# Small transform units made inside the matmul stretch of a last-stage chunk, in mid-step

## The chip, the cores and the metric

The kernel runs on one core of a Trainium2 chip. The metric is the device time of one execution in microseconds (us); a kernel's number is the median of its runs. A profile is one more execution, recorded instruction by instruction. TensorE (PE) multiplies matrices, VectorE (DVE) and ScalarE (ACT) do elementwise work and read the accumulators (PSUM), GpSimd (POOL) does elementwise work on the on-chip memory (SBUF) and issues DMAs, SyncE (SP) issues DMAs.

## The reference

The input is `x` of shape (8, 3008, 256). Along the sequence axis it is convolved with a filter given in the frequency domain, and the result goes through a two-layer network with a hard-swish:

```python
X = np.fft.rfft(x, axis=1)
y = np.fft.irfft(X * (filt_r + 1j * filt_i)[None], n=3008, axis=1)   # (8, 3008, 256)
h = y.reshape(8 * 3008, 256) @ w_in                                  # 256 -> 2048
out = (h * np.clip(h + 3, 0, 6) / 6) @ w_out                         # 2048 -> 256
```

All of it is float32.

## The kernel before

**The main loop.** The 24064 tokens are cut into 47 blocks of 512, and the 2048 hidden columns into 8 slices. A *step* is one (block, slice) pair; step i is slice i mod 8 of block i // 8, so there are 376. From block 1 on a step is an up projection (`up_1` to `up_5`, seven products of 128x128 by 256 columns, line L764), the activation (`relu` on ScalarE, L809; `hswish` on VectorE, L814), sums of activations (`g_sums` and `g_last`, L821, L822 and L827 on VectorE), and the down projection of the step before (`down`, L843). The products run with fewer multiplications by sums of operands; `t_sums` (L760) makes those sums of a block's tokens with seven GpSimd instructions. Around a block's end the accumulators `po` are combined: `out_1` (ScalarE), `out_2` (L909) and `out_3` (L914) in the step whose number is a multiple of 8, `out_4` (L918, L919 and one GpSimd sum) and `out_5` (L923) in the step after it. `out_3` waits for the last product of its step.

**The order within a step** is written out by hand. After `up_1` comes place 0 of the plan, then `hswish` of the second half of the step before, `g_sums`, `down(1)`, `up_2`, `down(2, 4)`, `up_3`, `down(5, 6)`, `up_4`, then place 1, `hswish` of the first half, `up_5` (with the second `relu`), `bi3_copies`, `down(7, 3)` and place 2. Each engine runs its instructions in the order in which they are written, so what stands earlier in this list also runs earlier on its engine.

**The transforms** of batches 1 to 7 are made beside the main loop, by units that a table `plan` hangs on steps and places:

- First stage: `a6_unit` (L480, place 1) turns six columns c at a time, in three *rounds* of four products; `a6_sums` (L495 to L498, VectorE, place 2) forms sums and differences, and `z6_store` (L505) writes them from GpSimd's queue. A batch has 32 columns: five sixes and a rest of two (`SIX`, `A_AT`). The rest has a single round and its own small tile.
- Second stage: `b_unit` (L539, place 0), `f_unit` (filter, VectorE, place 2), `y_unit` (L571, L572, VectorE with both operands in SBUF, place 2).
- Inverse: `bi3_unit` (place 1) takes three `y` tiles in three rounds (L599); its copies are on ScalarE (L602, L609) and VectorE (L601, L610), and `g3_store` writes from GpSimd's queue.
- Last stage: `n_five` (L704, place 0) makes a *chunk* of five columns with 40 small products, `ring` (L686, ScalarE) copies it into the ring `xn` of tokens, and `ready` calls `t_sums` when a block of tokens is full. `n_unit` makes smaller chunks.

**Quarters.** The products of these units use 64 rows by 64 columns of the array. Four of them, one on each quarter of the array, make a round. [...]In units of three rounds a third tile shares the bank `be`: one row half writes its part in the first round, the other in the third, and a tiny VectorE copy of two elements (L483, L601) stands between them, because the other half's product waits for it. Each float32 product shows as two records in the profile.

`psF` has two banks (the units' `psf` and the chunks' `psn`), `be` and `al` one each; `be` is also used by every step's up projection. `t3p` has one buffer (the three-tile result of `a6_unit` and `bi3_unit`), `t1p` two, `yp` three.

Of the kernel before, what the change touches and what calls it, by code (L numbers as in the profile page):

```python
# [10 lines left out]
FP32 = mybir.dt.float32  # L11
I32 = mybir.dt.int32
AXT = mybir.ActivationFunctionType
ALU = mybir.AluOpType
# [23 lines left out]
HC = NC // 2  # L38
XC = 4
NB = HC // XC  # L40
SIX = tuple(range(0, HC, 6))
TC = 4
NT = KH // TC
TB = 3
# [138 lines left out]
def kernel(  # L183
# [198 lines left out]
    def x_at(b, c):  # L382
        if b == 1:
            return xs[:, (b * NB + c) % 3, :, :], c * XC, XC
        t = xs.rearrange("p i j d -> p (i j) d")
        return t[:, ds((b * len(SIX) + c) % 2 * 6, 6), :], SIX[c], min(6, HC - SIX[c])

    def x_load(b, c):
        t, c0, n_ = x_at(b, c)
# [70 lines left out]
    def a_sums(b, c):  # L460
# [5 lines left out]
        nc.vector.tensor_tensor(out=t[:, :, 1, :], in0=t[:, :, 0, :], in1=ps, op=ALU.subtract)  # L466
        nc.vector.tensor_tensor(out=t[:, :, 0, :], in0=t[:, :, 0, :], in1=ps, op=ALU.add)

    def a6_unit(b, c):
        xc, c0, n = x_at(b, c)  # L470
        n //= 2
        t = t3p.tile([P, 3, 2, D], FP32, name="t3") if n == 3 else t1p.tile([P, 2, 2, D], FP32, name="t1")
        banks = [psF.tile([P, 512], FP32, name="psf", tag="f") for h in range(2)]
        be = psU.tile([P, 512], FP32, name="be") if n == 3 else None
        for r in range(n):
            for g in range(2):
                for h in range(2):
                    j, ps, o = (2, be, h) if r == 2 - 2 * h and n == 3 else (r - h if n == 3 else 0,) + (banks[h], r - h if n == 3 else 0)
                    q = g * n + j
                    nc.tensor.matmul(ps[ts(g, 64), ts(o, D)], wa[ds(h * 64, NA), ds((c0 + q) * 2 * KH, 64)],  # L480
                                     xc[ds(h * 64, NA), q, :], start=True, stop=True)
            if n == 3 and r == 0:
                nc.vector.tensor_copy(out=t[:, 2, 1, 0:2], in_=be[:, D:D + 2])  # L483
        m = min(n, 2)
        two = [ps[:, 0:m * D].rearrange("p (j d) -> p j d", d=D) for ps in banks]
        nc.scalar.activation(out=t[:, 0:m, 0, :], in_=two[0], func=AXT.Copy)
        if n == 3:
                nc.scalar.activation(out=t[:, 2, 1, 2:D], in_=be[:, D + 2:], func=AXT.Copy)
        st["t1", b, c] = t, be, two[1], n

    def a6_sums(b, c):
        t, be, ps, n = st["t1", b, c]
        v, m = nc.vector, min(n, 2)
        if n == 3:
            v.tensor_tensor(out=t[:, 2, 0, :], in0=be[:, 0:D], in1=t[:, 2, 1, :], op=ALU.add)  # L495
            v.tensor_tensor(out=t[:, 2, 1, :], in0=be[:, 0:D], in1=t[:, 2, 1, :], op=ALU.subtract)
        v.tensor_tensor(out=t[:, 0:m, 1, :], in0=t[:, 0:m, 0, :], in1=ps, op=ALU.subtract)
        v.tensor_tensor(out=t[:, 0:m, 0, :], in0=t[:, 0:m, 0, :], in1=ps, op=ALU.add)  # L498

    def z6_store(b, c):  # L500
        t, _, _, n = st.pop(("t1", b, c))
        for g in range(2):
            for ri in range(2):
                p0 = g * 64 + ri * KH
                nc.gpsimd.dma_start(z_d[b, :, ri, ds(SIX[c] + n * g, n), :, :].rearrange("k j s d -> k (j s d)"),  # L505
                                    t[p0:p0 + KH, 0:n, :, :].rearrange("p j s d -> p (j s d)"))

    def z_store(b, c, q=nc.gpsimd):
# [80 lines left out]
    def bi3_unit(b, i):  # L589
        ys = [st.pop(("y", b, i + v)) for v in range(3)]  # L590
        c = psU.tile([P, 512], FP32, name="be")
        banks = [psF.tile([P, 512], FP32, name="psf", tag="f") for ri in range(2)]
        t = t3p.tile([P, 3, 2, D], FP32, name="t3")
        to = [t[:, q, :, :].rearrange("p u d -> p (u d)") for q in range(3)]
        for r in range(3):
            for v in range(2):
                for ri in range(2):
                    x, u, ps, o = (2, v, c, ri) if r == 2 * ri else (v, r - 1 + ri, banks[ri], r - 1 + ri)
                    nc.tensor.matmul(ps[ts(v, 64), ts(o, D)], wi[ts(ri, 64), 0, :], ys[x][ts(ri, 64), u, :], start=True, stop=True)  # L599
            if r == 0:  # L600
                nc.vector.tensor_copy(out=to[2][:, 0:2], in_=c[:, 0:2])  # L601
        nc.scalar.activation(out=to[1], in_=banks[1], func=AXT.Copy)  # L602
        st["t3", b, i] = t
        st["bi3"] = to[0], banks[0], to[2], c

    def bi3_copies():
        if "bi3" in st:
            to, ps, third, c = st.pop("bi3")
            nc.scalar.activation(out=to, in_=ps, func=AXT.Copy)  # L609
            nc.vector.tensor_copy(out=third[:, 2:512], in_=c[:, 2:512])  # L610
# [81 lines left out]
            t_sums(t // PAIRS)  # L692


    def n_five(i):
        b, js, o, n = chunks[i]
        s0 = i % 2 * NJ
        ps = [psF.tile([P, 512], FP32, name="psn", tag="f")[:, 0:2 * n].rearrange("p (e n) -> p e n", e=2) for c in range(2)]
        for q, j in enumerate(js):
            for dh in range(2):  # L700
                for g in range(2):
                    for c in range(2):
                        r = ds(c * HALF, ATOM)
                        nc.tensor.matmul(ps[c][ts(g, HALF), dh, ts(q, NA)], t4[r, s0 + q, ds(dh * P + g * HALF, HALF)],  # L704
                                         groups[r, j, :], start=True, stop=True)
        for c in range(2):
            ring(i, 0, n, o, lambda at_: xn[:, :, c, at_], ps[c])
        ready(i)

    def n_unit(i, dh):  # L710
        ps = psF.tile([P, 512], FP32, name="psn", tag="f")
# [261 lines left out]
    EARLY = (a_unit, b_unit, bi_unit, n_unit, n_five)  # L973

    def at(step, fn, *a):
        plan.setdefault((step, 0 if fn in EARLY else 1 if fn in (w_scale, bi3_unit, a6_unit) else 2), []).append((fn, a))

    with tc.manual_schedule():

# [131 lines left out]
        in_block = {}  # L1111
        for i in range(2, len(chunks)):
            in_block.setdefault(pair(i)[0] // PAIRS, []).append(i)
        stored = 0
        for i in range(2, len(chunks)):
            k = pair(i)[0] // PAIRS
            head = chunks[i][2] == 0
            same = in_block[k]
            at_, kind = same.index(i) + 1 if len(same) > 1 else 0, kinds.get(k - 1, "a")
            steps = N_FIRST[k - 1][at_] if k - 1 in N_FIRST else (FIVE_AT[kind][at_],) * 2 if len(chunks[i][1]) == NJ else N_AT[kind][at_]  # L1120
            if head and len(same) == 1:
                steps = (6, 6)
            s0, s1 = ((k - 1) * NP + s for s in steps)
            five = len(chunks[i][1]) == NJ
            n_at[i] = s1
            if head:
                stored = s0 - 3 + (k == first[1])
            at(max(stored, n_at[i - 2] + 1), t4_load, i)
            if five:
                at(s1, n_five, i)  # L1130
                continue
            at(s0, n_unit, i, 0)
            at(s1, n_unit, i, 1)
# [1 line left out]

        A_AT = (4, 6, 10, 12, 14, 15)

        def places(n):  # L1140
            if n == 1:
                return (list(range(2, NB + 2)), [12, 13, 14, 18, 19, 20, 22, 23, 26, 27, 29, 31],
                        [13, 15, 16, 19, 21, 22, 24, 25, 28, 30, 30, 32], [17, 24, 30, 34])
            k = first[n] * NP
            a_at = [k - 7 * NP + i for i in A_AT]
            f_at, y_at, bi_at = ([k - (5 - 2 * r) * NP + i for r in range(2) for i in p]
                                 for p in ((2, 3, 6, 7, 12, 13), (4, 5, 10, 11, 14, 15), (11, 16)))
            return a_at, f_at, y_at, bi_at

        at(n_at[TAIL - 2] + 1, lambda: nc.sync.dma_start(edge, wai_d[:, ds(NW + ND, ND)]))  # L1150
# [2 lines left out]
        for n in range(1, B):  # L1153
            a_at, f_at, y_at, bi_at = places(n)
            for c, s in enumerate(a_at):
                at(s, a_unit if n == 1 else a6_unit, n, c)
                at(s, a_sums if n == 1 else a6_sums, n, c)
                at(s, *((z_store, n, c, nc.sync) if n == 1 else (z6_store, n, c)))
                if c >= (3 if n == 1 else 2):
                    at(max(a_at[c - 3 + (n > 1)], s - 6), x_load, n, c)  # L1160
                elif n > 1:
                    at(max(prev[-1 if n == 2 else c - 2], s - 6), x_load, n, c)
# [5 lines left out]
            for i in range(NU):  # L1168
                if i % 2 == 0 or n == 1:
                    at(f_at[i], b_unit, n, i)  # L1170
                if i % 3 == 0:
                    at(bi_at[i // 3], bi3_unit, n, i)
                    at(bi_at[i // 3], g3_store, n, i)
                at(y_at[i], y_unit, n, i)
            for i in range(NU):
                at(f_at[i], f_unit, n, i)
            prev = a_at

        HEAVY = (f_unit, y_unit, a_sums, n_five, a6_sums, bi3_unit)

        def late(i):
            return i % NP in (1, 2) or any(fn in HEAVY for place in range(3) for fn, a in plan.get((i - 1, place), ()))
# [103 lines left out]
```

## Time and profile before

| | |
|---|---|
| median of 3 runs | 2643.08 us (2642.48 to 2643.17) |
| the profiled execution | 2642.37 us, of which the span from first to last instruction is 2640.5 us |
| granted TensorE clock | 1.000 |
| busy: PE, DVE, ACT, POOL | 2626.3, 2046.7, 1296.5, 485.5 us |

From the trace's timeline of TensorE one reads the length of each step, from the start of its first up product to that of the next step's. From step 36 on (the steady part):

| what hangs on the step | steps | length, us |
|---|---|---|
| nothing | 207 | 6.148 to 6.149 |
| `b_unit` | 36 | 7.365 |
| `a6_unit`, a six | 18 | 7.879 to 7.883 |
| `a6_unit`, the rest of two | 6 | 6.936 to 6.937 |
| `bi3_unit` | 15 | 7.855 to 7.858 |
| `n_five` | 22 | 7.656 to 7.753 |
| `n_five` and a six | 12 | 9.387 to 9.390 |
| `n_five` and `bi3_unit` | 7 | 9.363 to 9.366 |

Numbers within a step are given as +x us from its start. How a line of the profile reads: line of the kernel, engine, operation, output<-inputs, shape, and count; then busy time and the mean of one, or, in a timeline, start and duration first and in brackets the engine's idle time before it with what ended it.

### The profile page before, as it was taken

What the parts mean: (1) busy time and instruction counts of PE and PEld (TensorE: products, weight loads), DVE (VectorE), ACT (ScalarE), POOL (GpSimd) and SP (SyncE); (2) the same over time, 40 slices, a digit from 0 to 9 for tenths busy, and PEclk for the clock granted to TensorE, in tenths of its full rate; (3) what the DMA queues carried; (4) which work ended last, traced back from release to release, by engine and by line L of the source; (5) the groups of instructions that cost most, each with busy time, mean ns of one, the idle gap of its engine ahead of it and who ended that gap; (6) DMA issues with size and microseconds to landing.
All of it is one profiled execution on the core that took longest, in us unless ns stands there. A gap on an engine that the chain in (4) does not pass through costs nothing.

```text
span 2640.5 us, 54927 instructions
## 1 busy us (share of the span) xinstructions
PE 2626.3 (99%) x21920; PEld 2338.3 (89%) x21920; DVE 2046.7 (78%) x3611; ACT 1296.5 (49%) x2677; POOL 485.5 (18%) x711
## 2 busy tenths in 40 slices
PE   9999999999999999999999999999999999999999
PEld 6698988989889998889988898888988889999998
DVE  7978867887678876788778887788877878766666
ACT  4554454444544445444454544545445454455554
POOL 2242021110211102121021210211112120111110
PEclk9999999999999999999999999999999999999999
DMA  9733234113341123411233112331223321110000
GB/s 247 222 85 83 55 103 112 53 32 85 81 113 53 36 81 85 109 53 36 81 89 105 53 37 80 89 104 53 58 61 88 104 56 48 48 43 23 19 21 25
DMA packets 130710, 198.29 MB, mean 75 GB/s; under 512 B 21602, under 2 KB 97472, under 8 KB 130262
## 3 DMA queue, kind: packets, MB, share of 16 engines
q1 hardware_dynamic: 115165, 150.12, 20.7%
q0 software_dynamic: 14720, 44.16, 6.1%
q8 instruction: 173, 2.83, 0.5%
q14 instruction: 83, 0.68, 0.1%
q10 hardware_dynamic: 569, 0.50, 0.1%
HBM read 122.43 MB, written 83.98 MB: 78 GB/s over the span
## 4 chain that ended last, share of the span: by engine, by line
PE 97%; DMA 1%; DVE 1%; issue 0%; ACT 0%; SPq 0%; POOL 0%; POOLq 0%; DVEq 0%; ACTq 0%
PE po L843 43%; PE al L764 24%; PE be L764 18%; PE psn L704 2%; PE psf L539 1%; PE psf L480 1%; PE po L886 1%; PE psf L599 1%; PE be L599 1%; PE be L480 1%; PE al L875 0%; PE be L875 0%; DMA ft<-in_filt_i_dram 0%; PE psf L453 0%; PE psn L715 0%; DMA wa<-wb_t 0%
## 5 line engine op out<-in xcount | busy, mean ns | idle before, releaser
L843 PEld LDWEIGHTS po<-w_all,g 128*128 128x128 f32 x10276 | 1370.3, 191 | 106.9 <-issue 10.4
L843 PE MATMUL po<-w_all,g 128*128 128x128 f32 x10276 | 1393.9, 276 | 1.0 <-DVE g L814 0.6
L809 ACT ACTIVATE r<-h,half_c 128x512 f32<-128x512 f32 x736 | 531.0, 721 | 334.3 <-DVE h L790 322.3
L764 PE MATMUL al<-xt,w_all 128*128 128x256 f32 x2208 | 659.6, 381 | 0.1
L814 DVE SCALAR_TENSOR_TENSOR g<-r,h 128x512 f32<-128x512 f32 x736 | 533.9, 727 | 147.6 <-ACT r L809 132.4
L764 PE MATMUL be<-xt,w_all 128*128 128x256 f32 x1472 | 437.8, 379 | 0.0
L790 DVE TENSOR_TENSOR h<-be,s 128x512 f32<-128x512 f32 x368 | 253.6, 689 | 144.8 <-PE be L764 136.2
L764 PEld LDWEIGHTS al<-xt,w_all 128*128 128x128 f32 x2208 | 335.4, 192 | 1.0 <-issue 0.5
L760 POOL TENSOR_TENSOR xt<-xn 128x256 f32<-128x256 f32 x184 | 149.7, 833 | 905.8 <-ACT xn L686 905.8
L764 PEld LDWEIGHTS be<-xt,w_all 128*128 128x128 f32 x1472 | 279.7, 190 | 37.9
L804 ACT ACTIVATE h<-al 128x256 f32<-128x256 f32 x368 | 141.4, 384 | 297.3 <-PE al L764 297.3
L795 DVE TENSOR_TENSOR h<-al,s 128x256 f32<-128x256 f32 x368 | 156.0, 424 | 156.2 <-PE al L764 154.3
L822 DVE TENSOR_TENSOR g<-g 128x512 f32<-128x512 f32 x367 | 261.4, 712 | 12.6
L785 ACT ACTIVATE s<-al 128x256 f32<-128x256 f32 x368 | 141.4, 384 | 214.4 <-PE al L764 212.9
L764 PE MATMUL al<-xn,w_all 128*128 128x256 f32 x736 | 226.4, 389 | 0.0
L776 ACT ACTIVATE s<-be 128x256 f32<-128x256 f32 x368 | 141.4, 384 | 171.0 <-PE be L764 171.0
L764 PE MATMUL be<-xn,w_all 128*128 128x256 f32 x736 | 218.9, 379 | 0.0
L821 DVE TENSOR_TENSOR g<-g 128x256 f32<-128x256 f32 x367 | 165.0, 450 | 12.6
L775 ACT ACTIVATE s<-al 128x256 f32<-128x256 f32 x368 | 141.1, 383 | 64.8 <-PE al L764 64.8
L827 DVE TENSOR_TENSOR g<-g 128x256 f32<-128x256 f32 x367 | 160.1, 436 | 2.4
L764 PEld LDWEIGHTS be<-xn,w_all 128*128 128x128 f32 x736 | 139.8, 190 | 18.9
L764 PEld LDWEIGHTS al<-xn,w_all 128*128 128x128 f32 x736 | 111.4, 191 | 24.7 <-issue 22.3
(170 smaller groups left out, 1850.0 us busy)
## 6 DMA issues: line engine op xcount, KB each, us to landing
t<-g_tmp SPq DMA_DIRECT2D x184, 120.0 KB
t<-z_tmp SPq DMA_DIRECT2D x42, 512.0 KB
g_tmp<-t POOLq DMA_DIRECT2D x68, 256.0 KB, 4.3
z_tmp<-t POOLq DMA_DIRECT2D x120, 144.0 KB, 3.5
o_tmp<-o SPq DMA_DIRECT2D x46, 256.0 KB
xs<-in_x_dram SPq DMA_DIRECT2D x60, 192.0 KB
ft<-in_filt_r_dram SPq DMA_DIRECT2D x168, 64.0 KB
ft<-in_filt_i_dram SPq DMA_DIRECT2D x168, 64.0 KB
```

The costliest lines, as they stand in the source:

```text
L760: nc.gpsimd.tensor_tensor(out=o, in0=x0, in1=x1, op=op_)
L764: nc.tensor.matmul(ps, w_in[p][:, w, :], x, start=start, stop=stop, skip_group_check=True)
L776: nc.scalar.activation(out=s5, in_=be[:, 1, :], func=AXT.Copy)
L785: nc.scalar.activation(out=s[:, 1, :], in_=al, func=AXT.Copy)
L790: nc.vector.tensor_tensor(out=st["h"][0].rearrange("p (a n) -> p a n", a=2), in0=be, in1=s, op=ALU.add)
L795: nc.vector.tensor_tensor(out=st["h"][1][:, 256:512], in0=al, in1=s5, op=ALU.add)
L809: nc.scalar.activation(out=r, in_=st["h"][i], func=AXT.Relu, bias=half_c, scale=1.0 / 6.0)
L814: nc.vector.scalar_tensor_tensor(out=st["g", k, p][:, o:o + 2, :].rearrange("p a n -> p (a n)"), in0=st["r", i], scalar=1.0, in1=st["h"][i ...
L821: v.tensor_tensor(out=g[:, G1, :], in0=g[:, G3, :], in1=g[:, G22, :], op=ALU.add)
L822: v.tensor_tensor(out=g[:, G3:G2 + 1:2, :], in0=g[:, G3:G1 + 1, :], in1=g[:, G11:G11 + 1, :].broadcast_to([P, 2, 256]), op=ALU.subtract)
L827: nc.vector.tensor_tensor(out=g[:, G4, :], in0=g[:, G12, :], in1=g[:, G2, :], op=ALU.subtract)
L843: nc.tensor.matmul(st["po", k][bank][:, part, u, :], g[:, a, ts(u, P)], w_out[p][:, w, :], start=(p == 0 and n in OPENS and u == 0), stop= ...
```

## The change

- `SIX` becomes 6, 6, 6, 6, 2, 6. The unit of two columns and, per batch of 2 to 7, three inverse units of a single `y` tile no longer have a stretch of their own: `five_and` makes each of them within the products of a chunk of five. In such a chunk one row half first makes two 256-column products of the small unit while the other row half makes eight products of the chunk; then both halves make twelve; then the roles are exchanged. Both halves of the small unit share the bank `be`, with the tiny VectorE copy (`order`) between.
- `five_and` stands at place 1 (before `up_5`), where the chunk alone stands at place 0. The ring copies, `ready` (and so `t_sums`) and the big VectorE copy of the inverse unit move to `bi3_copies`, behind `up_5`.
- Per batch of 2 to 7, four `bi3_unit` become three, and three single units are new (`BI_AT`). `A_AT` puts the first-stage units on offsets 4, 6, 8, 10, 12, 14 (before: 4, 6, 10, 12, 14, 15) from a step that is a multiple of 8. In the last batch one `y_unit` goes one step later.
- In `a6_unit` and `bi3_unit` the two products of one row half now follow each other within a round, and the half that writes `be` comes first in the first round and last in the third.

```diff
-SIX = tuple(range(0, HC, 6))
+SIX = (0, 6), (6, 6), (12, 6), (18, 6), (24, 2), (26, 6)
...
+    def a_product(ps, g, o, xc, c0, q, h):
+        nc.tensor.matmul(ps[ts(g, 64), ts(o, D)], wa[ds(h * 64, NA), ds((c0 + q) * 2 * KH, 64)],
+                         xc[ds(h * 64, NA), q, :], start=True, stop=True)
+
     def a6_unit(b, c):
...
         for r in range(n):
+            for h in (1, 0):
+                for g in range(2):
+                    j, ps, o = (2, be, h) if r == 2 - 2 * h else (r - h, banks[h], r - h)
+                    a_product(ps, g, o, xc, c0, g * n + j, h)
+            if r == 0:
+                nc.vector.tensor_copy(out=t[:, 2, 1, 0:2], in_=be[:, D:D + 2])
...
+    def a2_parts(b, c):
+        xc, c0, n = x_at(b, c)
+        t = t1p.tile([P, 2, 2, D], FP32, name="t1")
+        be = psU.tile([P, 512], FP32, name="be")
+        st["t1", b, c] = t, be, None, 1
+
+        def part(h):
             for g in range(2):
...
+                a_product(be, g, h, xc, c0, g, h)
+
+        def order():
+            nc.vector.tensor_copy(out=t[:, 0, 1, 0:2], in_=be[:, D:D + 2])
+
+        def copies():
+            nc.scalar.activation(out=t[:, 0, 1, 2:D], in_=be[:, D + 2:], func=AXT.Copy)
+        return 1, part, order, copies, lambda: None
...
         for r in range(3):
-            for v in range(2):
-                for ri in range(2):
+            for ri in range(2):
+                for v in range(2):
...
+    def bi1_parts(b, i):
+        y = st.pop(("y", b, i))
+        t = st["t3", b, i] = t1p.tile([P, 2, 2, D], FP32, name="t1")
+        be = psU.tile([P, 512], FP32, name="be")
...
+        def part(ri):
+            for v in range(2):
+                nc.tensor.matmul(be[ts(v, 64), ts(ri, D)], wi[ts(ri, 64), 0, :], y[ts(ri, 64), v, :], start=True, stop=True)
+
+        def order():
+            nc.vector.tensor_copy(out=to[:, 0:2], in_=be[:, 0:2])
+
+        def copies():
+            nc.vector.tensor_copy(out=to[:, 2:512], in_=be[:, 2:512])
+        return 0, part, order, lambda: None, copies
...
     def bi3_copies():
+        if "five" in st:
+            for f in st.pop("five"):
+                f()
...
-    def n_five(i):
+    def n_five(i, parts=None, b_=0, x=0):
...
+        order = [(q, dh, g) for q in range(NJ) for dh in range(2) for g in range(2)]
...
+        def both(a, b, n):
+            for i in range(n):
+                for c, o in ((0, a), (1, b)):
+                    product_(c, *order[o + i])
+
+        def rings():
+            for c in range(2):
+                ring(i, 0, n, o, lambda at_: xn[:, :, c, at_], ps[c])
+            ready(i)
+
+        if parts is None:
+            both(0, 0, len(order))
+            rings()
+            return
+        r, part, sync, copies, last = parts(b_, x)
+        part(r)
+        for m in range(8):
+            product_(1 - r, *order[m])
+        sync()
+        both(8 * r, 8 - 8 * r, 12)
+        part(1 - r)
+        for m in range(12, 20):
+            product_(r, *order[m])
+        copies()
+        st["five"] = last, rings
+
+    def five_and(*a):
+        n_five(*a)
...
-        A_AT = (4, 6, 10, 12, 14, 15)
+        BI_AT = {2: ((9, 0, 1), (14, 1, 3), (16, 4, 1), (25, 5, 1), (27, 6, 3), (32, 9, 3)),
+                 6: ((9, 0, 1), (14, 1, 3), (16, 4, 1), (17, 5, 1), (27, 6, 3), (32, 9, 3)),
+                 7: ((9, 0, 1), (11, 1, 1), (16, 2, 1), (17, 3, 3), (27, 6, 3), (32, 9, 3))}
+        A_AT = (4, 6, 8, 10, 12, 14)
...
+            bi_at = [(k - 5 * NP + s, i, m) for s, i, m in BI_AT.get(n, BI_AT[2])]
+            y_at[5] += n == B - 1
...
+        for s, i in five_at.items():
+            at(s, *((five_and, i) + with_five[s] if s in with_five else (n_five, i)))
...
-        HEAVY = (f_unit, y_unit, a_sums, n_five, a6_sums, bi3_unit)
+        HEAVY = (f_unit, y_unit, a_sums, n_five, five_and, a6_sums, bi3_unit)
```

## The prediction

> **What bounds the kernel now.** I read the engines' shares first, then the chain of waits, then the costliest groups.
>
> ```profile
> PE 2626.3 (99%) x21920; PEld 2338.3 (89%) x21920; DVE 2046.7 (78%) x3611; ACT 1296.5 (49%) x2677; POOL 485.5 (18%) x711
> PE 97%; DMA 1%; DVE 1%; issue 0%; ACT 0%; SPq 0%; POOL 0%; POOLq 0%; DVEq 0%; ACTq 0%
> L843 PE MATMUL po<-w_all,g 128*128 128x128 f32 x10276 | 1393.9, 276 | 1.0 <-DVE g L814 0.6
> ```
>
> TensorE is busy all the time and makes 97% of the chain. So a change pays by what it takes out of TensorE's row of products, and it costs where a product has to wait. VectorE is at 78%: in a step with added work it can become late. The timeline of TensorE gives a price for each unit; here the step with the unit of two columns:
>
> ```profile
> 736.74 0.60 PE L764 MATMUL al<-xt,w_all 128*128 128x256 f32 x2
> ...
> 741.65 0.66 PE L480 MATMUL psf<-xs,wa 47*64 47x256 f32 x8
> 742.25 0.70 PE L764 MATMUL al<-xn,w_all 128*128 128x256 f32 x2
> ...
> 743.67 0.60 PE L764 MATMUL al<-xt,w_all 128*128 128x256 f32 x2
> ```
>
> The step lasts 6.936 us, a bare one 6.148: the unit costs 0.788. Record by record, a 256-column record occupies its quarter for 0.216, so the round's own work is 0.432; the rest, 0.356, is going into quarters and out again. In the same way a chunk costs 7.656 - 6.148 = 1.508: twenty rounds of records at 0.0583 are 1.166, the rest is 0.342. A chunk and a six in one step cost 3.241 = 1.508 + 1.733: two stretches, paid twice.
>
> **Gains.** (1) Removed per batch of 2 to 7: the unit of two (0.788) and one `bi3_unit` (7.857 - 6.148 = 1.709). Over six batches: 14.98 us.
>
> (2) Added: 24 small units inside chunks. In the first part one half makes two 256-column products (0.432 per quarter) beside eight chunk products, four per quarter, 4 x 2 x 0.0583 = 0.467. Then twelve each, 0.700, then 0.467 again: 1.634 in place of 1.166, so 0.467 more. The lower end is the products' own 0.432. For the upper end there is a rule against the change. The Trainium skill ("TensorE: Matmul & The Clock Gate", The mechanism, in Part 3) says that products start and end strictly in the order of issue. Then the eight products behind two long ones could not start before the second long record, and each part would take 0.22 to 0.27 longer: some 0.95 per unit, 11.6 us more in all. The trace speaks otherwise: in a six's first round the second record of the first quarter starts 0.267 after its first, but the other three quarters start 0.007 to 0.020 after it. A quarter runs behind its own records alone. I take 0.467: 24 x 0.467 = 11.21 us.
>
> (3) Third rounds. In a `bi3_unit` the last rounds' records in `be` start 1.398 after the last full product, their neighbour at 1.335; in a six 1.417 and 1.335. So the wait for the tiny VectorE copy costs 0.063 and 0.082 a unit (lower end of the gain: nothing; upper: all of it). In the new order `be` is first in round one and last in round three, which is two places of 0.0067 for the inverse and four for the six; the weights, not loaded ahead behind a wait (0.051), stay exposed. I take 0.020 and 0.026: 22 x 0.020 + 30 x 0.026 = 1.2 us.
>
> (4) Chunks alone in a step last up to 7.753 because `t_sums` slows the `g_last` in the same step. The converted ones lose this excess over 7.656: 0.4 us.
>
> Gains: 14.98 - 11.21 + 1.2 + 0.4 = 5.4 us.
>
> **Losses.** All come from VectorE and ScalarE getting work later, and each is a wait of TensorE. The price of a wait: with `g_last` ended at +7.104 in step 121, the product due at +7.208 ran 0.051 late, so a product runs 0.155 after its operand. These are the VectorE instructions around a block's end (steps 80 and 81, which starts at 638.09):
>
> ```profile
> 637.40 0.68 DVE L909 TENSOR_TENSOR o<-po,p 128x512 f32<-128x512 f32 x1
> 638.29 0.42 DVE L914 TENSOR_TENSOR o<-po,o 128x256 f32<-128x256 f32 x1 [0.21 <-PE po L843]
> 638.63 0.68 DVE L814 SCALAR_TENSOR_TENSOR g<-r,h 128x512 f32<-128x512 f32 x1
> ...
> 640.42 0.42 DVE L918 TENSOR_TENSOR o<-po,o 128x256 f32<-128x256 f32 x1
> 640.75 0.41 DVE L919 TENSOR_TENSOR o<-po,o 128x256 f32<-128x256 f32 x1
> ```
>
> and these a six's sums, in steps 84 and 85 (from 665.31):
>
> ```profile
> 664.42 0.42 DVE L495 TENSOR_TENSOR t<-be,t 128x256 f32<-128x256 f32 x1 [0.58 <-ACT t L488]
> 664.88 0.42 DVE L496 TENSOR_TENSOR t<-be,t 128x256 f32<-128x256 f32 x1
> 665.22 0.68 DVE L497 TENSOR_TENSOR t<-t,psf 128x512 f32<-128x512 f32 x1
> 665.93 0.69 DVE L498 TENSOR_TENSOR t<-t,psf 128x512 f32<-128x512 f32 x1
> 666.53 0.68 DVE L814 SCALAR_TENSOR_TENSOR g<-r,h 128x512 f32<-128x512 f32 x1
> ```
>
> (5) The new offset 8 in `A_AT` puts a six on a step that is a multiple of 8, where `out_2` and `out_3` stand; none stood there. `out_3` waits for the step's last product and ends at +0.62 of the next step. The sums are queued behind it: 2.12 us from first to last start and the next, so `hswish` starts at +2.66 in place of +0.54 and ends at +3.34. `down(2)`, due at +2.61, runs at 3.50: 0.89 late. `g_sums` ends at 4.5, `out_4` at 5.2, and `down(5)` must not overwrite the `po` that `out_4` reads: it runs at 5.36, due at 3.93 + 0.89 = 4.82, so 0.54 more. The sum for the other half of h comes behind it and holds `up_5` by some 0.05. Together 1.48 per batch: 8.9 us. Cover that remains: none, since the next step has `out_4` and `out_5` of its own.
>
> (6) Ring copies behind the second `relu`. In step 112 that `relu` starts 0.27 before the next step. Ring copies start 0.62 and 1.08 after it, each holding ScalarE 0.46, so the copy of `al` starts at +1.26 (normally +0.63) and ends at +1.64. `up_2` overwrites `al` at +1.74 and needs it ended at 1.59: 0.06 late. It's the same in 22 steps (two have a `b_unit` between); in five the chunk wraps round the ring, with twice the copies and 0.08 more. 1.6 us.
>
> (7) `t_sums` starts behind the ring copies, at +1.4 of the next step instead of +3.9 of the chunk's own. What it does to VectorE, in steps 121 and 122:
>
> ```profile
> 917.55 1.60 POOL L760 TENSOR_TENSOR xt<-xt 128x256 f32<-128x256 f32 x2
> ...
> 917.77 0.79 DVE L827 TENSOR_TENSOR g<-g 128x256 f32<-128x256 f32 x1
> 918.49 2.35 DVE L814 SCALAR_TENSOR_TENSOR g<-r,h 128x512 f32<-128x512 f32 x2
> 920.87 0.83 DVE L821 TENSOR_TENSOR g<-g 128x256 f32<-128x256 f32 x1
> ```
>
> Two SBUF operands cost 0.79 instead of 0.42, and 1.19 instead of 0.69; operands from PSUM aren't slowed. The seven sums last 5.8 to 6.05. Before, step 122 bore this without a wait (6.148 long). Now they end at +7.3, so `g_last` and `hswish` of the step behind the chunk are slowed (`hswish` ends near +6.6), and a `y_unit` at its end too: two instructions of 0.69 become 1.1 each, and the next `hswish` ends at +2.9 of the step after. `down(2)` runs at 3.04, due at 2.61: 0.43. This meets offset 10 in five batches and 26 in four: 9 x 0.43 = 3.9 us. The Trainium skill ("SBUF — State Buffer", SBUF: two separate sides) calls the shared port an exclusive lock, the loser blocked for a whole instruction. A slowed VectorE instruction would then lose up to the 0.73 of a GpSimd sum, not the row's 0.38 to 0.50: four such in a row make 1 us more per place, 9 in all. I take the row. Without a `y_unit` the slowed work has room (`hswish` due by +2.45).
>
> (8) In the last batch `y_unit` 5 moves to step 304, behind `out_2` and `out_3` and into the `t_sums` of a chunk; as in (5), with 1.7 us of `y` ahead of a slowed `hswish`: 2.1 us, once.
>
> Losses: 8.9 + 1.6 + 3.9 + 2.1 = 16.5 us. DMAs: each six still has four steps (over 25 us) between its load and its use, and stores wait some 4 us to land; GpSimd's queue issues two more stores per batch, behind `t_sums`. I put these at nothing.
>
> **Sum.** 16.5 - 5.4 = +11.1 us. On the profiled execution: 2642.37 + 11.1 = 2653.5 (span 2651.6). The median of the runs stands 0.71 above that execution, so 2643.08 + 11.1 = 2654.2. A difference under 0.2% (5.3 us) isn't told from none.
>
> **Rivals.** (A) VectorE catches up and no product waits: then 5.4 us faster, 2637.7. It is decided where `hswish` ends in the step after a six at offset 8: before +2.45 there is no wait. For it: 78% busy means 1.3 us spare per step; against it: `out_3` can't run before +0.20 and the sums are behind it. 4%. (B) Only (5) is real, since the steps after chunks have spare time: 2643.08 + 8.9 - 5.4 = 2646.6, no difference told. For it: step 122 took slowed sums without a wait; against it: no `y_unit` stood in them. 9%. (C) Long and short products don't run beside each other, as in the rule of (2): 2654.2 + 11.6 = 2665.8. Against it speak the 0.007 between quarters. 5%. (D) The upper ends of (3), 2.7 us lower, belong to the main case.
>
> **How the numbers follow.** Main case 82%: 2654.2, by (3) down to 2651.5, and by (6) and (7), read half or one and a half times, 2.8 either way: 2649 to 2659. Taking up the two near cases in part gives the range 2648.5 to 2659.5. Faster by over 0.2%: most of A, which ends at that bound, 3%. Within 0.2%: B and the rest of A, 10%. Slower: the main case and C, 87%.
>
> **What the next profile would show.** Step 41 and each like it (48 later) near 7.62 us where a bare one has 6.148, with `hswish` starting at +2.66: (5) right; under 6.4, wrong. Chunks with a small unit at 8.12 us: (2) right; at 8.6, rival C. Bare steps right behind them at 6.21: (6). Steps 59 and 75 with 0.4 us more than bare or `bi3_unit` steps: (7). What would make it wrong above all is VectorE's real order around step 40, as 54% of the losses lie there.

## The result and the profile after

The changed kernel takes 2657.82 us (median of 4 runs, 2657.29 to 2658.17); the kernel before, run beside it, 2643.12 us (2642.48 to 2643.34). The ratio is 1.0056, with a 95% interval of 1.0038 to 1.0073: 14.7 us slower. The profiled execution took 2658.08 us, with a span of 2656.3 us and a granted clock of 1.000.

The page of the changed kernel: engines, the chain of waits, and two groups of products (the last figures of a group are TensorE's idle time ahead of them and what ended it). The last line is the second of these groups in the kernel before.

```profile
PE 2629.0 (99%) x21920; PEld 2348.6 (88%) x21920; DVE 2072.6 (78%) x3641; ACT 1282.3 (48%) x2665; POOL 505.6 (19%) x723
...
PE 94%; DVE 3%; DMA 2%; issue 0%; ACT 0%; SPq 0%; POOL 0%; DVEq 0%; POOLq 0%; ACTq 0%
...
L910 PE MATMUL po<-w_all,g 128*128 128x128 f32 x10276 | 1393.0, 276 | 6.6 <-DVE g L881 5.1
...
L831 PE MATMUL be<-xn,w_all 128*128 128x256 f32 x736 | 219.4, 380 | 5.8 <-DVE t L512 5.8
...
L764 PE MATMUL be<-xn,w_all 128*128 128x256 f32 x736 | 218.9, 379 | 0.0
```

TensorE still reads 99%, so this line tells nothing. The chain tells that VectorE now holds products up: it has gone from 1% to 3%. It is too coarse to tell how much (it reads 3% in the first experiment's kernel too, whose steps are 8.7 us shorter). The groups name the waits. The down products (L910, before L843) wait 6.6 us in place of 1.0, for `hswish` (L881) above all. A wait that did not exist before stands at the second up product of a step, on `be`: 5.8 us, for a six's sums (L512).

The lengths of the steps, read as before, say where the time went (from step 8 on they add up to 14.57 us; what lies ahead of step 8 is the same code, and took 126.0 to 128.5 us in the profiles of this study, with no relation to the change):

| term of the prediction | predicted, us | from the step lengths, us |
|---|---|---|
| 1, units removed | -14.98 | -14.98 |
| 2, small units in chunks | +11.21 | +12.54 (18 x 0.518, steps of 8.174; 6 x 0.536, of 8.192) |
| 3, third rounds | -1.2 | -1.94 (22 x 0.024, 30 x 0.047) |
| 4, chunks alone | -0.4 | -0.4 |
| 5, six on offset 8 | +8.9 | +8.67 (six steps of 7.591 to 7.595, 6.148 bare) |
| 6, steps behind chunks | +1.6 | +1.4 (17 x 0.037, 5 x 0.158) |
| 7, `y_unit` under `t_sums` | +3.9 | +5.65 (59 and four more: 0.57 to 0.59; 75 and three more: 0.69) |
| 8, last batch's `y_unit` | +2.1 | +2.08 (step 305: 9.909) |
| not predicted | | +1.57 (steps 259, 301: 0.69 and 0.74; 300: 0.13; 258: 0.01) |
| sum | +11.1 | +14.6 |

This is VectorE at the first such place of term 5, in the timeline of the changed kernel; step 41 starts at 367.01.

```profile
365.47 0.68 DVE L976 TENSOR_TENSOR o<-po,p 128x512 f32<-128x512 f32 x1
367.21 0.42 DVE L981 TENSOR_TENSOR o<-po,o 128x256 f32<-128x256 f32 x1 [1.06 <-PE po L910]
367.55 0.42 DVE L511 TENSOR_TENSOR t<-be,t 128x256 f32<-128x256 f32 x1
368.00 0.42 DVE L512 TENSOR_TENSOR t<-be,t 128x256 f32<-128x256 f32 x1
368.35 0.68 DVE L514 TENSOR_TENSOR t<-t,psf 128x512 f32<-128x512 f32 x1
369.06 0.69 DVE L515 TENSOR_TENSOR t<-t,psf 128x512 f32<-128x512 f32 x1
369.66 0.68 DVE L881 SCALAR_TENSOR_TENSOR g<-r,h 128x512 f32<-128x512 f32 x1
```

And TensorE in the same step:

```profile
367.01 0.60 PE L831 MATMUL al<-xt,w_all 128*128 128x256 f32 x2
368.57 0.67 PE L831 MATMUL be<-xn,w_all 128*128 128x256 f32 x2 [0.97 <-DVE t L512]
...
372.25 1.16 PE L910 MATMUL po<-w_all,g 128*128 128x128 f32 x8
```

VectorE stands idle for 1.06 us before `out_3` (L981), which waits for step 40's last product; the sums stand behind it, and `hswish` starts at +2.65. All of this is as predicted. But the first product that is late is another: the second of the step (its third record), due at +0.434 and running at +1.563. It overwrites `be`, which the first two sums read. `down(2)` then is no later than that.

Term 7 in step 59, which starts at 490.755 (VectorE, the GpSimd sums beside it, and the late down product on TensorE):

```profile
489.08 0.50 DVE L894 TENSOR_TENSOR g<-g 128x256 f32<-128x256 f32 x1
...
489.50 1.21 DVE L881 SCALAR_TENSOR_TENSOR g<-r,h 128x512 f32<-128x512 f32 x1
...
490.12 1.18 POOL L827 TENSOR_TENSOR xt<-xn 128x256 f32<-128x256 f32 x1
...
490.74 1.11 DVE L588 TENSOR_TENSOR y<-s 64x512 f32<-64x512 f32 x1
...
491.38 1.06 POOL L827 TENSOR_TENSOR xt<-xt 128x256 f32<-128x256 f32 x1
...
491.88 1.10 DVE L589 TENSOR_TENSOR y<-s 64x512 f32<-64x512 f32 x1
...
493.10 0.69 DVE L881 SCALAR_TENSOR_TENSOR g<-r,h 128x512 f32<-128x512 f32 x1
...
493.84 1.16 PE L910 MATMUL po<-w_all,g 128*128 128x128 f32 x8 [0.32 <-DVE g L881]
```

The last instruction of step 58's `g_last`, `hswish` and both of `y_unit` are slow, and the next `hswish` ends at +3.03. The down product, due at +2.607, starts at +3.088.

### The profile page after: what moved, and what is told of

It reads as the page before. It is cut to its first block, busy times and chain, and to the rows that moved or that the text cites. A ratio compares the mean times of both kernels' runs of the same rounds, so it can differ in the third digit from the quotient of the medians.

```text
span 2656.3 us, 54912 instructions
## 1 busy us (share of the span) xinstructions
PE 2629.0 (99%) x21920; PEld 2348.6 (88%) x21920; DVE 2072.6 (78%) x3641; ACT 1282.3 (48%) x2665; POOL 505.6 (19%) x723
## 4 chain that ended last, share of the span: by engine, by line
PE 94%; DVE 3%; DMA 2%; issue 0%; ACT 0%; SPq 0%; POOL 0%; DVEq 0%; POOLq 0%; ACTq 0%
PE po L910 42%; PE al L831 24%; PE be L831 17%; PE psn L745 2%; PE psf L556 1%; DVE g L881 1%; PE po L953 1%; PE psf L470 1%; PE be L470 1%; PE psf L616 1%; PE be L616 1%; DVE y L588 1%; DMA w_all<-in_x_dram 1%; DVE y L589 0%; DMA g_tmp<-t 0%
## 5 line engine op out<-in xcount | busy, mean ns | idle before, releaser
L910 PEld LDWEIGHTS po<-w_all,g 128*128 128x128 f32 x10276 | 1370.0, 191 | 119.1 <-DVE g L888 17.6
L910 PE MATMUL po<-w_all,g 128*128 128x128 f32 x10276 | 1393.0, 276 | 6.6 <-DVE g L881 5.1
L881 DVE SCALAR_TENSOR_TENSOR g<-r,h 128x512 f32<-128x512 f32 x736 | 533.4, 725 | 159.6 <-ACT r L876 145.0
L889 DVE TENSOR_TENSOR g<-g 128x512 f32<-128x512 f32 x367 | 268.1, 731 | 12.6
L827 POOL TENSOR_TENSOR xt<-xn 128x256 f32<-128x256 f32 x184 | 160.9, 894 | 543.7 <-ACT xn L728 507.7
L843 ACT ACTIVATE s<-be 128x256 f32<-128x256 f32 x368 | 141.7, 385 | 167.8 <-PE be L831 167.8
L987 POOL TENSOR_TENSOR o<-p,o 128x256 f32<-128x256 f32 x46 | 37.3, 812 | 734.8 <-PE be L831 406.1
```

What stands on the lines that cost most here:

```text
L827: nc.gpsimd.tensor_tensor(out=o, in0=x0, in1=x1, op=op_)
L843: nc.scalar.activation(out=s5, in_=be[:, 1, :], func=AXT.Copy)
L881: nc.vector.scalar_tensor_tensor(out=st["g", k, p][:, o:o + 2, :].rearrange("p a n -> p (a n)"), in0=st["r", i], scalar=1.0, in1=st["h"][i ...
L889: v.tensor_tensor(out=g[:, G3:G2 + 1:2, :], in0=g[:, G3:G1 + 1, :], in1=g[:, G11:G11 + 1, :].broadcast_to([P, 2, 256]), op=ALU.subtract)
L910: nc.tensor.matmul(st["po", k][bank][:, part, u, :], g[:, a, ts(u, P)], w_out[p][:, w, :], start=(p == 0 and n in OPENS and u == 0), stop= ...
```

## The experiments

Each comparison is with the kernel before, run beside it on the same chip (its medians lie between 2642.70 and 2643.24). Of what the trace gives beside the times, "step sum" is the difference of the steps' lengths from step 8 on; it leaves out the changing time ahead of step 8, and is finer than the medians.

### Sixes off the steps that are multiples of 8

```diff
-        A_AT = (4, 6, 8, 10, 12, 14)
+        A_AT = (4, 6, 9, 11, 12, 14)
```

> The changed kernel with the sixes of offsets 8 and 10 put on 9 and 11, so that none stands on a step that is a multiple of 8. Theory (term 5: the six's VectorE sums queue behind out_3, which waits for the last product of such a step): the step after the six falls from 7.59 to near a bare 6.15 us, six times 1.44 = 8.7 us less: about 2649.1 us. Rival (VectorE is late after any six that comes this early in the batch, wherever it stands): the steps behind offsets 9 or 11 grow instead and the time stays at about 2657.8 us.

Measured: 2648.64 us, ratio 1.0022 (1.0013 to 1.0031). The step sum is 8.67 less than that of the changed kernel. A six on step 41, and then step 42 (from 372.36) in this kernel's timeline, VectorE and TensorE:

```profile
371.54 0.42 DVE L511 TENSOR_TENSOR t<-be,t 128x256 f32<-128x256 f32 x1 [0.63 <-ACT t L488]
372.00 0.42 DVE L512 TENSOR_TENSOR t<-be,t 128x256 f32<-128x256 f32 x1
...
372.80 0.59 PE L831 MATMUL be<-xn,w_all 128*128 128x256 f32 x2
```

The sums of `be` now end 0.06 after the step's start instead of 1.41, and the product on `be` runs on time. The step behind the six is 6.148 long. The rival falls: the six is harmless one step later.

### Only one six on offset 8, in the kernel before

```diff
-        A_AT = (4, 6, 10, 12, 14, 15)
+        A_AT = (4, 6, 8, 12, 14, 15)
```

> The kernel before with the sixes put on offsets 4, 6, 8, 12, 14, 15 (one that stood on 10 now on 8) and nothing else. Theory (term 5 needs nothing else of the change): step 41 and its like become about 7.6 us long in place of 6.15, six times 1.44 = 8.7 us more than before: about 2651.8 us. Rival (the wait needs the new chunks, which stand on offset 9 and load VectorE): no wait, about 2643.1 us.

Measured: 2651.51 us, ratio 1.0034 (1.0021 to 1.0048). Step 41 and its like are 7.596 to 7.599 long, and nothing else changes: step sum +8.75. So term 5 needs no other part of the change.

### The six on offset 8, with its sums ahead of `out_3`

```diff
+                sums_first = any(fn is a6_sums for fn, a in plan.get((i, 2), ()))
+                if sums_first:
+                    do(2)
                 if pd == NP - 1 or ends:
                     out_3(kd)
+                if sums_first:
+                    continue
             do(2)
```

> The changed kernel with the sixes left on offset 8, but there the six's VectorE sums (a6_sums) are written ahead of out_3 instead of behind it. In the changed kernel the first product that is late in step 41 is not down(2) but the third product of the step, be, by 1.129 us: it overwrites the bank that the first two sums read, and these stand behind out_3. Theory (it is the order behind out_3 that costs, not the six on such a step): the sums run before the step's end as in any other step, be isn't late, and step 41 and its like fall from 7.59 to near 6.15, 8.7 us less, 2649.1 us; if the new block's first down products (due at +1.30) have to wait for the po that out_3, now ending at about +1.65, still reads, 0.4 to 0.5 of each returns, and it is about 6 us less, 2651.8 us. Rival (VectorE has too much work in these two steps in whatever order): the wait only changes its place, 2657.8 us.

Measured: 2651.39 us, ratio 1.0031 (1.0019 to 1.0043); step sum 6.2 less than the changed kernel's. Step 41 (from 366.42) lasts 6.564. VectorE and TensorE there, in the timeline:

```profile
366.05 0.42 DVE L512 TENSOR_TENSOR t<-be,t 128x256 f32<-128x256 f32 x1
...
367.71 0.42 DVE L981 TENSOR_TENSOR o<-po,o 128x256 f32<-128x256 f32 x1
...
370.17 0.41 DVE L986 TENSOR_TENSOR o<-po,o 128x256 f32<-128x256 f32 x1
```

```profile
366.86 0.59 PE L831 MATMUL be<-xn,w_all 128*128 128x256 f32 x2
...
369.92 0.60 PE L831 MATMUL al<-xt,w_all 128*128 128x256 f32 x2
370.64 1.16 PE L910 MATMUL po<-w_all,g 128*128 128x128 f32 x8
```

(The product that the expectation calls the third is the step's second; its record is the third.) With the same work in the same steps and only the order turned round, `be` runs on time: it was the place behind `out_3` that cost 1.03 of the 1.44. The second case expected gave the right size, but not the right place. The first down products are on time. What is left, 0.415, arises at `down(5)`, which has to wait for `out_4` (L986) to read `po`: 0.279 at its first record, 0.104 more at its second, 0.03 at the second record of `up_5`. VectorE has much to do in these two steps, and in both orders tried it is late there; that no order avoids it is not shown. The prediction had seen this link (its 0.54).

### The third and ninth `y_unit` one step earlier

```diff
-                          for p in ((2, 3, 6, 7, 12, 13), (4, 5, 10, 11, 14, 15)))
+                          for p in ((2, 3, 6, 7, 12, 13), (4, 5, 9, 11, 14, 15)))
```

> The changed kernel with the third and the ninth y_unit of a batch one step earlier, in the step of a chunk instead of the step behind it, and so ahead of that chunk's t_sums. Theory (term 7: t_sums slow the y_unit's two instructions and the hswish behind them): steps 59, 75 and their like fall by 0.57 to 0.69 us, and 258/259 and 300/301 stay: about 5.6 us less, 2652.2 us. Rival (VectorE is simply full around chunks, and the y_unit delays hswish in whichever step it stands): the loss moves one step forward and the time stays at about 2657.8 us.

Measured: 2651.72 us, ratio 1.0034 (1.0022 to 1.0047), step sum 5.6 less than the changed kernel's. Steps 59, 107, 155, 203, 251 are bare again (6.148), and 75 and its like are 7.834; 258/259 and 300/301 stay. The same two instructions, in the chunk's own step, make nothing late.

### Short sums of the tokens

```diff
-        t = xtp.tile([P, 5, PAIRS], FP32, name="xt")
+        t = st["xt", k - 2] if k > 5 else xtp.tile([P, 5, PAIRS], FP32, name="xt")
+        w = 32 if k > 5 else 256
...
-            nc.gpsimd.tensor_tensor(out=o, in0=x0, in1=x1, op=op_)
+            nc.gpsimd.tensor_tensor(out=o[:, 0:w], in0=x0[:, 0:w], in1=x1[:, 0:w], op=op_)
```

> The changed kernel with t_sums working on 32 of its 256 columns from the seventh block on, in the same places (so most of the token sums of these blocks are left out). Theory (term 7 and what was missed beside it: GpSimd's sums slow VectorE's instructions with two SBUF operands): steps 59, 75 and their like, 258/259 and 300/301 lose their excess (5.65 + 1.57 us), chunks alone fall from about 7.69 to 7.656 (0.4 us), and step 305 falls from 9.91 to 8.3 to 8.6 since its y_unit still stands behind out_3 (about 1.4 us): 9.0 us less, about 2648.8 us. Rival (the y_unit and f_unit make VectorE late by their place alone): only the 0.4 us of the chunks go, about 2657.4 us.

Measured: 2649.15 us, ratio 1.0024 (1.0015 to 1.0033), step sum 8.5 less than the changed kernel's. VectorE in steps 58 and 59 in the timeline (step 59 from 490.846; this kernel's lines stand one later from L822 on):

```profile
489.50 0.69 DVE L882 SCALAR_TENSOR_TENSOR g<-r,h 128x512 f32<-128x512 f32 x1
490.22 0.69 DVE L588 TENSOR_TENSOR y<-s 64x512 f32<-64x512 f32 x1
490.94 0.69 DVE L589 TENSOR_TENSOR y<-s 64x512 f32<-64x512 f32 x1
491.74 0.69 DVE L882 SCALAR_TENSOR_TENSOR g<-r,h 128x512 f32<-128x512 f32 x1
```

VectorE's program and its places are unchanged, and every instruction is back at 0.69; steps 59, 75 and their like, 259 and 301 lose all of their excess (5.65 and 1.43 us), and chunks alone fall to 7.656. So it is GpSimd's sums, not the place of `y_unit` and `f_unit`. Step 300 keeps its 0.13, and step 305 loses 1.15 of 2.08: the 0.92 that stay are its `y_unit` behind `out_3`, as in term 5. The expectation had 0.5 to 0.8 there.

### The last batch as before

```diff
-                 7: ((9, 0, 1), (11, 1, 1), (16, 2, 1), (17, 3, 3), (27, 6, 3), (32, 9, 3))}
+                 7: ((11, 0, 3), (16, 3, 3), (27, 6, 3), (32, 9, 3))}
...
-            y_at[5] += n == B - 1
```

> The changed kernel with the last batch's inverse units and y_unit as before the change (three bi3_units of three tiles more, no single ones; no y_unit a step later). Theory (term 8, and the f_unit of steps 300/301 caught by t_sums): steps 300, 301 and 305 lose 0.13, 0.74 and 2.08 us; three single units (3 x 0.52) and their ring copies (0.04 each) go and one bi3_unit (1.685) comes: about 2.9 us less, 2654.9 us. Rival (the y_unit of that batch is late in either place, in step 303 too): 2657.8 us.

Measured: 2653.80 us, ratio 1.0041 (1.0029 to 1.0054); step sum 2.75 less than the changed kernel's. Step 305 is 6.149, 301 is 6.148, 300 is 7.365. The loss of term 8 is gone with the two edits together; how it divides between `y_unit`'s place and the sums is told by the short sums above (0.92 and 1.15). The rest of the median's difference (4.0) lies within the spread of single runs (2653.4 to 2655.6).

### Three repairs together

The edits of the first, the `y_unit` and the last-batch experiment in one kernel.

> The changed kernel with the sixes on offsets 9 and 11, the third and ninth y_unit a step earlier, and the last batch's inverse as before. Theory (terms 5, 7 and 8 are independent waits, and nothing else is lost but term 6 and step 259): 2657.8 - 8.7 - 5.6 - 2.9 = 2640.6 us, near the kernel with the new order of rounds alone. Rival (a wait removed in one place returns in the next, so that the repairs don't add): 2644 us or more.

Measured: 2640.91 us, ratio 0.9992 (0.9983 to 1.0001). The step sum is -1.96 against the kernel before and -16.53 against the changed one, where the three alone give 8.67 + 5.59 + 2.75 = 17.0. They add to within 0.5, and what goes against it is 0.64 in one place, step 58: there an `hswish` and the first of `t_sums` start together and `hswish` starts 0.35 later than its operands allow. It happened in one step of this kernel alone, and its cause stays open.

### The new order of rounds alone

```diff
-            for g in range(2):
-                for h in range(2):
+            for h in ((1, 0) if n == 3 else (0, 1)):
+                for g in range(2):
...
-            for v in range(2):
-                for ri in range(2):
+            for ri in range(2):
+                for v in range(2):
```

> The kernel before with the new order of products within the rounds of a6_unit and bi3_unit alone. Theory (term 3, with the sizes that the profile after shows: 0.047 per six, 0.024 per bi3_unit): 30 x 0.047 + 28 x 0.024 = 2.1 us less than before, 2641.0 us. With the sizes predicted (0.026 and 0.020) it is 1.3 us, 2641.8 us. Rival (the shorter stretches owe their length to something else in the changed kernel): 2643.1 us.

Measured: 2640.63 us, ratio 0.9993 (0.9984 to 1.0002), step sum -2.02. Every six is 7.833 to 7.836 (before 7.879 to 7.883) and every `bi3_unit` 7.833 to 7.836 (before 7.855 to 7.858). The times alone can't tell it from no change; the steps can.

### Six, and ten, products beside the long ones

```diff
-        for m in range(8):
+        for m in range(6):
             product_(1 - r, *order[m])
         sync()
-        both(8 * r, 8 - 8 * r, 12)
+        both(6 * r, 6 - 6 * r, 14)
         part(1 - r)
-        for m in range(12, 20):
+        for m in range(14, 20):
```

> The changed kernel with six instead of eight chunk products beside each pair of long products, and fourteen instead of twelve pairs in between. A chunk with a small unit cost 0.518 us more than a chunk, 0.051 more than the 0.467 of term 2. If that comes from the eight products running past the long ones (0.467 against 0.432), the chunk's step falls from 8.174 towards 8.12, up to 1.2 us in all: 2656.6 us. If it comes from one quarter falling a record behind where long and short products meet, whatever their number, it stays at 8.17 or, by 0.05 for the longer middle part, rises to 8.22: 2657.8 to 2659.0 us.

The other has 10 where this one has 6, and 10 where it has 14:

> The changed kernel with ten instead of eight chunk products beside each pair of long products, and ten instead of twelve pairs in between. With six, the last pair of long products began at 1.280 and 1.339 of the stretch instead of 1.222 and 1.279, and the chunk's step grew from 8.174 to 8.234. Theory (the half that has no long products runs ahead of the other by a few products only and is then held, so each pair fewer beside them costs a record of 0.058, and each pair more saves one until the other half ends last): the last pair begins at about 1.164 and 1.222; the end of the other half, 1.705, then ends the stretch in place of 1.741, and the step of a chunk with an inverse unit falls by 0.036 to 8.138, that with two columns by less: 18 x 0.036 + 6 x 0.01 = 0.7 us less, 2657.1 us. Rival (eight is the best split since ten products run longer past the long ones, 0.583 against 0.432): 8.22 or more, 2658.8 us.

Measured: six 2657.95 us, ratio 1.0057 (1.0043 to 1.0070), step sum 1.22 more than the changed kernel's; ten 2658.95 us, ratio 1.0060 (1.0047 to 1.0072), step sum 1.39 more. The stretch of step 112 in the three timelines of TensorE, from the first long record to the next full product; first the changed kernel (eight):

```profile
860.86 0.43 PE L631 MATMUL be<-y,wi 64*64 64x256 f32 x2
860.87 0.44 PE L745 MATMUL psn<-wai,t 48*64 48x47 f32 x8
861.12 0.38 PE L631 MATMUL be<-y,wi 64*64 64x256 f32 x1
...
862.08 0.41 PE L631 MATMUL be<-y,wi 64*64 64x256 f32 x1
...
862.14 0.41 PE L631 MATMUL be<-y,wi 64*64 64x256 f32 x1
...
862.69 0.48 PE L831 MATMUL al<-xn,w_all 128*128 128x256 f32 x1
```

Six:

```profile
859.79 0.43 PE L631 MATMUL be<-y,wi 64*64 64x256 f32 x2
...
861.08 0.41 PE L631 MATMUL be<-y,wi 64*64 64x256 f32 x1
...
861.13 0.41 PE L631 MATMUL be<-y,wi 64*64 64x256 f32 x1
...
861.69 0.48 PE L831 MATMUL al<-xn,w_all 128*128 128x256 f32 x1
```

Ten:

```profile
861.19 0.43 PE L631 MATMUL be<-y,wi 64*64 64x256 f32 x2
...
862.64 0.40 PE L631 MATMUL be<-y,wi 64*64 64x256 f32 x2
862.67 0.48 PE L745 MATMUL psn<-wai,t 48*64 48x47 f32 x9
863.09 0.48 PE L831 MATMUL al<-xn,w_all 128*128 128x256 f32 x1
```

In the first fence eight short records start between the long products' first records and the second: long and short products do run beside each other. The stretches last 1.83 (eight), 1.90 (six) and 1.90 us (ten), and the chunk's step is 8.174, 8.234 and 8.235. With six, the second long pair starts about a record later (1.29 and 1.34 into the stretch, eight 1.22 and 1.28); with ten it starts no later, but the short records of the other half go on past it. So eight is the best of the three, and each of the others costs one record (0.06; with six, the chunks with the two columns cost only 0.025 more). The overrun of the short products is not the cause of the 0.051 that was missing in term 2, and the idea that each pair more beside the long ones saves a record fell too. With eight, one quarter's second long product starts 0.057 behind the other's, which is about what is missing; that it is the cause is not shown, and why it is behind stays open.

### The unit of two columns alone, and with ten

The kernel before with the new order of rounds, the unit of two columns in a chunk, and the sixes on 9 and 11; the inverse units and `y_at` as before the change.

```diff
-SIX = tuple(range(0, HC, 6))
+SIX = (0, 6), (6, 6), (12, 6), (18, 6), (24, 2), (26, 6)
...
-        A_AT = (4, 6, 10, 12, 14, 15)
+        A_AT = (4, 6, 9, 11, 12, 14)
```

> The kernel before with the new order of rounds, the unit of two columns inside a chunk, and the sixes on offsets 4, 6, 9, 11, 12, 14; the inverse units as before the change (no single ones, no y_unit moved). Theory (the parts add): new order -2.1; six units of two, 6 x (0.536 + 0.037 - 0.788) = -1.3; no wait behind sixes or y_units: 3.4 us less than before, 2639.6 us. Rival (waits return once the sixes stand on 9 and 11 beside the chunk on offset 12 with its unit): 2641 us or more.

Measured: 2639.48 us, ratio 0.9988 (0.9979 to 0.9997), step sum -3.32. By its steps it is the shortest kernel of this study; the times alone don't tell it from the one with the new order. From its page:

```profile
PE 97%; DMA 1%; DVE 1%; ACT 0%; issue 0%; SPq 0%; POOL 0%; POOLq 0%; DVEq 0%; ACTq 0%
...
L910 PE MATMUL po<-w_all,g 128*128 128x128 f32 x10276 | 1393.2, 276 | 1.0 <-DVE g L881 0.6
```

The chain and the down products' idle time are those of the kernel before: no wait behind a six or a `y_unit` has come back. Only `up_2` behind the chunk is still 0.034 late (term 6).

> The kernel of the two columns alone with ten instead of eight chunk products beside the long ones. Only six stretches differ. Theory of the record that is saved: up to 0.04 each, 0.1 to 0.2 us less; rival: 0.05 each more. Both lie within what the times can tell, so the step's length in the trace (8.192 with eight) decides.

Measured: 2639.96 us, ratio 0.9989 (0.9981 to 0.9998); the six steps with two columns are 8.253 to 8.255 instead of 8.193. The rival's size, as with the inverse units.

## Why the prediction was right, and where it was not

The sign and the mechanism were right: the losses are VectorE's queue (terms 5, 7, 8), and they outweigh the gains. The measured 2657.82 us lies in the range given, 2648.5 to 2659.5, in its upper part. By the steps the prediction was 3.5 us short (11.1 against 14.6): term 2 cost 1.3 more, term 7 1.75 more and 1.57 was not foreseen, while term 3 gained 0.74 more and terms 5 and 6 cost 0.4 less.

- **Terms 1 and 4** hold. **Term 3** was sized too low: 0.024 and 0.047 a unit in place of 0.020 and 0.026, between the value taken and the upper end (0.063 and 0.082). +0.74 us of gain.
- **Term 2** was right in its mechanism, 0.05 to 0.07 short in size: 0.518 and 0.536 against 0.467, 1.3 us. The rule of the Trainium skill ("TensorE: Matmul & The Clock Gate", Part 3, The mechanism) on the strict order of products would have made it 0.95; eight short records that start ahead of the second long one, and 0.518, speak against it here. Rival C is out. The 0.05 is about one record (0.058); where it comes from is open.
- **Term 5** was right in its sum (8.67 against 8.9), but its path was wrong at the first link. The prediction let `hswish` hold `down(2)` for 0.89. What was held is the product on `be`, 1.129 late and 0.074 more at its second record; both facts were on the table (the first two sums read `be`, and each step's up projection writes it), and were not put together. Then `out_4` held `down(5)` for 0.101 + 0.104, and 0.034 followed at `up_5`: 1.443. The prediction's 0.89 + 0.54 + 0.05 came to nearly the same by luck. The order of `out_3` and the sums decides 1.03 of it; 0.415 stays when it is turned round. The price of a wait, 0.155, was read at a product whose first record ran on time (+7.210); its second was the one that ran 0.051 late. It served all the same, since it is the sum of what the two records lose (last section).
- **Term 6** holds: 0.037 in place of 0.06, 0.158 in place of 0.14 where the chunk wraps round.
- **Term 7** was mis-sized: 0.585 and 0.69 in place of 0.43, 1.75 us in all. The `y` instructions took 1.1 each, as predicted, but the prediction's own figures (`hswish` ending at +6.6, two of 1.1, one of 0.69, less a step of 6.2) give an end near +3.3, not the +2.9 that it used. In the trace the slowed `hswish` ends at +6.26 and the next one at +3.03 (step 59) and +3.14 (step 75). A slowed instruction lost 0.42 (`y_unit`) or 0.52 (`hswish`), about as in the row that the prediction took (0.38 to 0.50). But the row is no evidence against the exclusive lock of the Trainium skill ("SBUF — State Buffer", SBUF: two separate sides), against which the prediction had set it: in the trace the two engines take turns, as that page says (last section). What an instruction loses is the part of the other's work that is still to come when its own could begin, and that was less than a whole sum (0.73).
- **Term 8** holds: 2.08 against 2.1.
- **What failed outright** is the sentence that without a `y_unit` the slowed work has room. At steps 258/259 and 300/301 an `f_unit` of three instructions stands in that place. In the changed kernel's timeline, step 259 starting at 1872.618:

```profile
1870.94 0.92 DVE L894 TENSOR_TENSOR g<-g 128x256 f32<-128x256 f32 x1
1871.79 1.21 DVE L881 SCALAR_TENSOR_TENSOR g<-r,h 128x512 f32<-128x512 f32 x1
1872.92 0.68 DVE L577 TENSOR_TENSOR s<-psf,ft 128x512 f32<-128x512 f32 x1
...
1875.04 0.69 DVE L881 SCALAR_TENSOR_TENSOR g<-r,h 128x512 f32<-128x512 f32 x1
```

Its own instructions, which read PSUM, are not slowed (0.68), but they start 0.3 into the next step behind a slowed `hswish`, and the next one ends at +3.1. The short sums removed this excess whole (1.43 us). The 0.14 of the two `b_unit` steps beside it is another wait, behind the ring copies (term 6): in step 300 the last of them ends at +1.471, and the `b_unit`'s product on that bank of `psF`, due at +1.397, runs at +1.524. Together 1.57 us.

Of the change itself little was to be had even without a wait. A `bi3_unit` costs 7.833 - 6.148 = 1.685 in the new order; the three single units that take its place cost 3 x 0.518 and three late `up_2` of 0.037, together 1.665. In five of the six batches one of the three stands in a chunk that wraps round the ring (0.158 in place of 0.037), and then they cost 1.786, more than what they replace. Only the unit of two columns pays, 0.788 - 0.536 - 0.037 = 0.215 per batch, and the new order of rounds, 2.0 in all. The kernel with these two alone has the shortest steps; the one with all parts and three repairs comes out level with the new order alone.

## What to carry to other kernels

Before a unit is moved, write down for its new step which instruction of each engine's queue waits for the step's end, and list every buffer that the instructions behind it still read: the first product that is late can be one that overwrites one of these (here +0.434 in the step), ahead of the one whose operand they make (+2.607). Cost "room" by every unit in the plan that can stand in that place, not by the kind that came to mind first. And work out what the piece would bring with no wait at all: here three small units in shared stretches cost as much as the one they replaced, or a little more.

## What the runs showed of the hardware

- A wait of a down product costs twice: its first record starts 0.05 to 0.06 after the recorded end of its operand, and its second, due 0.110 later, starts 0.213 later (step 59: 2.607 and 2.717 became 3.088 and 3.301). The same 0.10 to 0.105 appears in steps 41, 75, 259, 301 and 305, and with the short sums in 305. The prediction's 0.155 was the sum of both.
- TensorE's busy time hides waits. Idle time ahead of the groups grew by 5.6 (down products) and 5.8 us (`be`), where the steps grew by some 19 us at the places of waits.
- VectorE's instructions with two operands in SBUF and GpSimd's sums take turns. From 100 to 2620 us of the changed kernel's trace, 179 such VectorE instructions are over 0.05 longer than their median. All but 4 of them end a fixed time after the end of a GpSimd sum: 0.545 to 0.560 us for 512 columns, 0.278 to 0.286 for 256. Of 163 sums longer than 0.78, 156 end 0.58 to 0.60 after the end of such a VectorE instruction. The lines of steps 58 and 59 show it: a sum ends at 490.12 + 1.18 = 491.30, the first instruction of `y_unit` at 491.85, the next sum at 492.44, the second of `y_unit` at 492.98. So while both queues are full, one of each takes 1.13 us together, and `y_unit`'s 0.69 becomes 1.10. Instructions with an operand in PSUM are not slowed (`f_unit` 0.68 to 0.70 in all 84 units).
